# The last 64 features of gate and up on two halves of the rows, and a main loop dealt out by hand

## The chip, the cores and the metric

The kernel runs on one core of one Trainium2 chip. The metric is the device time of one execution in microseconds (us). A core has a matrix engine (TensorE, "PE" in the profile, with its weight loads as "PEld"), a vector engine (VectorE, "DVE"), a scalar engine (ScalarE, "ACT"), GpSimd ("POOL") and SyncE ("SP", which here only issues transfers). TensorE writes its results to PSUM, eight banks of 512 float32 values on each of 128 rows; ScalarE and VectorE move them from there to the on-chip memory.

## The reference

The kernel computes the output of a block and its gradients with respect to the inputs and weights. The block is an adaptive layer norm, a filter in the frequency domain, a second adaptive layer norm, and a gated layer without a nonlinearity:

```python
h = _layernorm(x) * (1 + ca) + sa
x = x + ga * irfft2(rfft2(h) * (w_r + 1j * w_i))
h = _layernorm(x) * (1 + cb) + sb
g = h @ w_gate; u = h @ w_up
x = x + gb * ((g * u) @ w_down)
```

There are 2048 tokens (16 tiles of 128), 576 features and 4608 hidden units (36 blocks of 128); data is bfloat16. The main loop belongs to the gated layer. With gh the gradient that comes back to the hidden units (grad_out scaled by gb, times w_down transposed), it computes g and u, then g * u, gh * u and gh * g, the three weight gradients, and the gradient of h.

## The kernel before

The program builds its instructions from Python loops; a scheduler then orders them by priority, which is program order unless said otherwise, and starts an instruction earlier when it is ready and others wait. Buffers come from pools with a fixed number of copies. A transfer is queued on SP or POOL, and each queue is worked off in order.

Before the main loop, the spectral stages and the product with w_down (u4p, L365) run. L495 makes h2p, the second normalised input with tokens on the rows; it has 640 columns, and L209 has filled the last 64 with zeros. L499 turns it by a transposing transfer into h2T: five blocks of 128 features on the rows, of which the fifth holds 64 features and 64 rows of zeros.

The main loop (L584 to L643) passes once over each of the 36 hidden blocks, fb. A pass has these parts:

- *gup* (L604 to L613): for four groups of 512 tokens and for gate and up, one PSUM bank is filled by five matmuls (L609), one for each block of features; the fifth has 64 rows of weights and 64 rows of zeros (L588). ScalarE copies the bank out (L610, gT and uT); VectorE makes hhT, ggT and guT (L611 to L613).
- *turn* (L614 to L620): hhT goes to memory, and three transposing transfers on SP (L619) make hh_sf, gg_sf and gu_sf, with tokens on the rows.
- *u57* (L548 to L569), for the block before: three weight gradients, each of two halves of 288 columns with 16 matmuls a half (L554), a copy by ScalarE (L556), and a store, for two of the three behind another transposing transfer (L561 to L563).
- *u8* (L627 to L640): for 16 token tiles and two halves, two matmuls (L635) and an addition by VectorE (L640) into a float32 sum. Pass 34 leaves this out, and pass 35 does both blocks, with four matmuls a bank.

So TensorE has 40 matmuls of 512 columns and 96 + 64 of 288 columns in a pass. PSUM is split three ways: three banks for gup, three for u8p, two for u57p. Weights of gate and up (wgu, two copies, each for two passes) come in on SP and POOL (L591, L592), the gradient ghh on POOL (L598), and turned weights wT every fourth pass (L578). The order of the parts on TensorE is the scheduler's: it mixes gup of the next pass with u8 of this one, and u57 runs in one piece. After the loop the two last blocks' u57 follow, among them the first matmuls of the next stage (L829), each tied behind an entry of the list "fill".

Of the kernel before, what the change touches and what calls it, by code (L numbers as in the profile page):

```python
# [9 lines left out]
FP32 = mybir.dt.float32  # L10
# [9 lines left out]
NT = 16  # L20
S = 2048
D = 576
# [60 lines left out]
def build(ctx, tc, A_x, A_w_r, A_w_i, B_w_gate, B_w_up, B_w_down, c_in, w_mod, grad_out,  # L83
# [103 lines left out]
    with ExitStack() as hs:  # L187
# [319 lines left out]
    with ExitStack() as ms:  # L507
# [13 lines left out]
        with ExitStack() as bs:  # L521
# [23 lines left out]
            nso = [0]  # L545
            fill = []

            def u57_product(sf, rhs_n):  # L548
                so = so4[:, nso[0] % NSO, :]
                nso[0] += 1  # L550
                for h in range(2):
                    pw = u57ps.tile([128, 512], FP32, name="u57p")
                    for t in range(NT):
                        mm = nc.tensor.matmul(pw[:, 0:288], lhsT=sf[:, t, :], rhs=rhs_n[:, t, h * 288:(h + 1) * 288], start=(t == 0), stop=(t == NT - 1))  # L554
                    fill.append(mm.ins)
                    nc.scalar.copy(so[:, h * 288:(h + 1) * 288], pw[:, 0:288])  # L556
                return so
# [7 lines left out]
            def emit_u57(fb_, sfs_):  # L565
                so = u57_product(sfs_[0], gon)
                nc.sync.dma_start(out_6[fb_ * 128:(fb_ + 1) * 128, :], so[:, 0:D])
                for sf, odst in ((sfs_[1], out_4), (sfs_[2], out_5)):
                    u57_turn(fb_, u57_product(sf, h2n), odst)  # L569

            def wT_load(f0, after):
                nb = min(FBT, NFB - f0)
# [6 lines left out]
                return wT  # L579

            wgu = None
            wTs = {}
            u8 = []
            for fb in range(NFB):  # L584
                if fb % FBW == 0:
                    nb = min(FBW, NFB - fb)
                    wgu = wp.tile([128, 2, 5, FBW * 128], BF, name="wgu")
                    nc.gpsimd.memset(wgu[64:128, :, 4, :], 0.0)  # L588
                    for wi_, wsrc in enumerate((B_w_gate, B_w_up)):
                        eng = nc.sync if wi_ == 0 else nc.gpsimd  # L590
                        eng.dma_start(wgu[:, wi_, 0:4, 0:nb * 128], wsrc[0:512, fb * 128:(fb + nb) * 128].rearrange("(m q) f -> q m f", q=128))  # L591
                        eng.dma_start(wgu[0:64, wi_, 4, 0:nb * 128], wsrc[512:576, fb * 128:(fb + nb) * 128])  # L592
                if fb == 0:
                    wTs[0] = wT_load(0, turns[-7:-2])
                jw = fb % FBW
                jt = fb % FBT
                ghh = ghp.tile([128, NT, 128], BF, name="ghh")
                nc.gpsimd.dma_start(ghh[:].rearrange("f t p -> f (t p)"), ghhT_d[fb * 128:(fb + 1) * 128, :])  # L598
                gT = tp2.tile([128, NT, 128], BF, name="gT")
                uT = tp2.tile([128, NT, 128], BF, name="uT")  # L600
                hhT = tp.tile([128, NT, 128], BF, name="hhT")
                ggT = tp.tile([128, NT, 128], BF, name="ggT")
                guT = tp.tile([128, NT, 128], BF, name="guT")
                for sb4 in range(4):  # L604
                    ts_ = slice(4 * sb4, 4 * sb4 + 4)
                    for wi_, dstT in enumerate((gT, uT)):
                        pt = gups.tile([128, 4, 128], FP32, name="gup")
                        for m in range(5):
                            nc.tensor.matmul(pt[:], lhsT=wgu[:, wi_, m, jw * 128:(jw + 1) * 128], rhs=h2T[:, ts_, m, :], start=(m == 0), stop=(m == 4))  # L609
                        nc.scalar.copy(dstT[:, ts_, :], pt[:])  # L610
                    nc.vector.tensor_tensor(out=hhT[:, ts_, :], in0=gT[:, ts_, :], in1=uT[:, ts_, :], op=MUL)  # L611
                    nc.vector.tensor_tensor(out=ggT[:, ts_, :], in0=ghh[:, ts_, :], in1=uT[:, ts_, :], op=MUL)
                    nc.vector.tensor_tensor(out=guT[:, ts_, :], in0=ghh[:, ts_, :], in1=gT[:, ts_, :], op=MUL)  # L613
                nc.gpsimd.dma_start(hhT_d[:, :, fb, :].rearrange("tp f x -> f tp x"), hhT[:].rearrange("f (tp ti) p -> f tp (ti p)", ti=2))  # L614
                sfs = []
                for nm, srcT in (("hh_sf", hhT), ("gg_sf", ggT), ("gu_sf", guT)):
                    sf = sfp.tile([128, NT, 128], BF, name=nm)
                    with tc.high_priority(-2 * HEAD_START if fb == NFB - 1 else 0):
                        turned = nc.sync.dma_start_transpose(out=sf[:], in_=srcT[:].rearrange("f t p -> f (t p)"))  # L619
                    sfs.append(sf)  # L620
                if fb % FBT == 1 and fb + 3 < NFB:
                    wTs[fb // FBT + 1] = wT_load(fb + 3, [turned.ins] * 5)
                wT = wTs[fb // FBT]
                if pend and fb < NFB - 1:
                    emit_u57(*pend.pop(0))
                u8.append((ggT, guT, wT, jt))
                for t in range(NT):  # L627
                    if fb == NFB - 2:
                        break
                    for h in range(2):  # L630
                        hs_ = slice(h * 288, (h + 1) * 288)
                        pu = u8ps.tile([128, 512], FP32, name="u8p")
                        mms = [(x[:, t, :], wt_[:, wi_, j_, hs_]) for gg_, gu_, wt_, j_ in u8 for wi_, x in enumerate((gg_, gu_))]
                        for k, (l_, r_) in enumerate(mms):
                            nc.tensor.matmul(pu[:, 0:288], lhsT=l_, rhs=r_, start=(k == 0), stop=(k == len(mms) - 1))  # L635
                        dst = acc(t)[:, hs_]
                        if fb == 0:
                            nc.vector.tensor_copy(dst, pu[:, 0:288])
                        else:
                            nc.vector.tensor_tensor(out=dst, in0=dst, in1=pu[:, 0:288], op=ADD)  # L640
                if fb != NFB - 2:
                    u8 = []
                pend.append((fb, sfs))  # L643
            fill.clear()
            for p in pend:
                emit_u57(*p)
        res2cm.__exit__(None, None, None)
        res3cm.__exit__(None, None, None)

# [506 lines left out]
```

## Time and profile before

| | us |
|---|---|
| median of 3 runs | 1622.52 |
| lowest, highest | 1619.5, 1630.39 |
| the profiled execution's own time | 1615.75 |
| its span, first to last instruction | 1614.0 |
| mean granted TensorE clock | 0.989 |

All lines of the profile are from that one execution. In the groups of instructions, a line names the source line, engine, operation, what is written and read, the shape and the count; then come the total busy time in us, the mean duration of one in ns, and the idle time of that engine just before such instructions with what ended it. Matmuls are pipelined, so their durations overlap: the sum over a group is not the time that it took, and the distance between two starts is. The main loop fills some 980 us of the span, from the first L609 at 280.0 us to the last at 1258.5.

### The profile page before, as it was taken

How to read it: one execution, taken by the hardware profiler on the slowest of the kernel's cores; microseconds unless marked ns; L12 is line 12 of the kernel's file. 1: busy time of each engine (PE TensorE's matmuls, PEld its weight loads, DVE VectorE, ACT ScalarE, POOL GpSimd, SP SyncE). 2: the span in 40 equal slices, each digit the busy share in tenths (PEclk: the TensorE clock that was granted, in tenths of full speed). 3: DMA queues.
4: the chain of work that ended last, by engine and by line, in shares of the span. 5: the costliest groups of instructions: out<-in, count | busy, mean ns of one | idle time of the engine just before them, and what ended most of it. 6: DMA issues, size and time to landing. Idle time of an engine off the chain costs nothing.

```text
span 1614.0 us, 29981 instructions
## 1 busy us (share of the span) xinstructions
PE 1558.2 (97%) x11354; PEld 1067.8 (66%) x11354; DVE 990.4 (61%) x2594; ACT 560.1 (35%) x1108; POOL 180.5 (11%) x303
## 2 busy tenths in 40 slices
PE   6999999999999999999999999999999889899996
PEld 4666644667666676766667676666767666677774
DVE  7766743674756657475665747566574765678655
ACT  6666722222222222222222222222222265565022
POOL 0002311101010100101010010101000011100232
PEclk9999999999999999999999999999999999999998
DMA  9978993777677685866867686786856686635774
GB/s 324 280 211 235 281 278 128 161 131 152 133 157 140 129 161 109 176 137 128 164 123 150 132 167 115 151 146 130 173 98 142 179 253 193 235 113 181 273 225 153
DMA packets 482996, 280.38 MB, mean 174 GB/s; under 512 B 405377, under 2 KB 450178, under 8 KB 481954
## 3 DMA queue, kind: packets, MB, share of 16 engines
q1 hardware_dynamic: 457666, 185.38, 53.2%
q0 software_dynamic: 25184, 93.07, 18.7%
q8 instruction: 89, 1.46, 0.4%
q14 instruction: 57, 0.47, 0.1%
HBM read 108.51 MB, written 82.31 MB: 118 GB/s over the span
## 4 chain that ended last, share of the span: by engine, by line
PE 81%; DMA 7%; DVE 5%; issue 3%; ACT 3%; SPq 0%; POOL 0%; ACTq 0%; DVEq 0%; POOLq 0%
PE u57p L554 26%; PE gup L609 19%; PE u8p L635 17%; PE u4p L365 9%; PE u3p L1056 2%; DMA Xn<-xn_d 2%; PE yp L472 1%; DMA n2c<-n_d 1%; DMA wdB<-in_B_w_down_dram 1%; PE zp L317 1%; DMA out_dram<-o 1%; PE zp L829 1%; PE yp L965 1%; DMA ghhT_d<-ghh_st 1%; DVE pr L746 1%
## 5 line engine op out<-in xcount | busy, mean ns | idle before, releaser
L640 DVE TENSOR_TENSOR acc<-acc,u8p 128x288 f32<-128x288 f32 x1088 | 429.5, 450 | 354.1 <-PE u8p L635 352.9
L609 PE MATMUL gup<-h2T,wgu 128*128 128x512 bf16 x1440 | 433.3, 379 | 0.6 <-ACT uT L610 0.6
L635 PE MATMUL u8p<-wT,ggT 128*128 128x288 bf16 x1152 | 315.0, 287 | 4.3 <-DVE acc L640 4.3
L635 PE MATMUL u8p<-wT,guT 128*128 128x288 bf16 x1152 | 315.1, 287 | 0.0
L609 PEld LDWEIGHTS <-wgu 128*128 128x128 bf16 x1440 | 140.8, 98 | 97.4 <-issue 0.8
L556 ACT CAST so<-u57p 128x288 bf16<-128x288 f32 x216 | 86.2, 399 | 328.5 <-PE u57p L554 324.3
L635 PEld LDWEIGHTS <-guT 128*128 128x128 bf16 x1152 | 112.8, 98 | 101.3 <-issue 4.7
L365 PE MATMUL u4p<-goT,wdT 128*128 128x512 bf16 x720 | 163.7, 382 | 2.7 <-ACT ghh_st L139 2.4
L610 ACT CAST gT<-gup 128x512 bf16<-128x512 f32 x144 | 84.4, 586 | 226.3 <-PE gup L609 226.3
L554 PE MATMUL u57p<-gon,hh_sf 128*128 128x288 bf16 x1152 | 151.0, 288 | 0.0
L610 ACT CAST uT<-gup 128x512 bf16<-128x512 f32 x144 | 84.4, 586 | 189.3 <-PE gup L609 186.7
L554 PE MATMUL u57p<-h2p,gu_sf 128*128 128x288 bf16 x1152 | 148.5, 286 | 0.0
L554 PE MATMUL u57p<-h2p,gg_sf 128*128 128x288 bf16 x1152 | 148.1, 286 | 0.0
L554 PEld LDWEIGHTS <-hh_sf 128*128 128x128 bf16 x1152 | 113.5, 99 | 35.8
L1056 PEld LDWEIGHTS <-hl 128*128 128x128 bf16 x1152 | 111.2, 98 | 35.9 <-issue 8.2
L635 PEld LDWEIGHTS <-ggT 128*128 128x128 bf16 x1152 | 112.9, 98 | 29.1
L554 PEld LDWEIGHTS <-gg_sf 128*128 128x128 bf16 x1152 | 112.5, 98 | 28.3
L554 PEld LDWEIGHTS <-gu_sf 128*128 128x128 bf16 x1152 | 112.5, 98 | 28.2
L365 PEld LDWEIGHTS <-wdT 128*128 128x128 bf16 x720 | 70.0, 98 | 80.9 <-issue 6.0
L1056 PE MATMUL u3p<-wdB,hl 128*128 128x288 bf16 x672 | 94.2, 287 | 7.0 <-DMA wdB<-in_B_w_down_dram 6.0
L614 POOL DMA_DIRECT2D hhT_d<-hhT x36 | 33.2, 922 | 502.8 <-DVE hhT L611 498.6
L611 DVE TENSOR_TENSOR hhT<-gT,uT 128x512 bf16<-128x512 bf16 x144 | 60.7, 421 | 29.5 <-ACT uT L610 27.1
(355 smaller groups left out, 1659.1 us busy)
## 6 DMA issues: line engine op xcount, KB each, us to landing
ghhT_d<-ghh_st POOLq DMA_DIRECT2D x36, 512.0 KB, 4.1
ghh<-ghhT_d POOLq DMA_DIRECT2D x36, 512.0 KB, 7.7
hhT_d<-hhT POOLq DMA_DIRECT2D x36, 512.0 KB, 6.7
hl<-hhT_d SPq DMA_DIRECT2D x32, 576.0 KB, 8.3
out_dram<-woT SPq DMA_DIRECT2D x72, 128.0 KB, 2.0
wdn<-in_B_w_down_dram SPq DMA_DIRECT2D x18, 288.0 KB, 3.7
out_dram<-so SPq DMA_DIRECT2D x36, 144.0 KB, 2.4
wgu<-in_B_w_gate_dram SPq DMA_DIRECT2D x18, 256.0 KB, 3.3
```

Source lines behind the costliest of these rows:

```text
L317: mm = nc.tensor.matmul(zp[:, :FP], lhsT=hTs[t][:, m, :], rhs=T["RD"][:, m, cc, :], start=(m == 0), stop=(m == 4))
L365: nc.tensor.matmul(pt[:], lhsT=wdTs[k][:, j, m, :], rhs=goT[:, 4 * sb4:4 * sb4 + 4, m, :], start=(m == 0), stop=(m == 4))
L472: nc.tensor.matmul(yp[:, 0:288], lhsT=ut[:, fc, cc * 128:(cc + 1) * 128], rhs=T["IR"][:, fc, cc, h * 288:(h + 1) * 288], start=(k == 0), s ...
L554: mm = nc.tensor.matmul(pw[:, 0:288], lhsT=sf[:, t, :], rhs=rhs_n[:, t, h * 288:(h + 1) * 288], start=(t == 0), stop=(t == NT - 1))
L556: nc.scalar.copy(so[:, h * 288:(h + 1) * 288], pw[:, 0:288])
L609: nc.tensor.matmul(pt[:], lhsT=wgu[:, wi_, m, jw * 128:(jw + 1) * 128], rhs=h2T[:, ts_, m, :], start=(m == 0), stop=(m == 4))
L610: nc.scalar.copy(dstT[:, ts_, :], pt[:])
L611: nc.vector.tensor_tensor(out=hhT[:, ts_, :], in0=gT[:, ts_, :], in1=uT[:, ts_, :], op=MUL)
L614: nc.gpsimd.dma_start(hhT_d[:, :, fb, :].rearrange("tp f x -> f tp x"), hhT[:].rearrange("f (tp ti) p -> f tp (ti p)", ti=2))
L635: nc.tensor.matmul(pu[:, 0:288], lhsT=l_, rhs=r_, start=(k == 0), stop=(k == len(mms) - 1))
L640: nc.vector.tensor_tensor(out=dst, in0=dst, in1=pu[:, 0:288], op=ADD)
L1056: mm = nc.tensor.matmul(p2[:, 0:288], lhsT=hls[fb // 9][:, fb % 9, ti * 128:(ti + 1) * 128], rhs=(wdA[:, fb] if fb < 15 else wdB[:, fb - 1 ...
```

## The change

**The fifth block on two halves of the rows.** The zeros in h2p are replaced by a second copy of features 512 to 575 (a VectorE addition of 64 columns beside L495), so that the fifth block of h2T holds these features on rows 0 to 63 and again on rows 64 to 127. The weights' tile becomes nine blocks: four of gate, four of up, and one in which gate's last 64 features lie on rows 0 to 63 and up's on rows 64 to 127. The fill of L588 goes.

**Four short matmuls open a batch of four banks.** A pass has two batches ("half" 0 and 1), each of two token groups for gate and up. A batch first issues four matmuls over 64 rows, one for each bank, gate and up in turn, and then for each bank the four whole blocks. Three banks come from gup's, the fourth from u57p's pool.

**The rest dealt by hand.** Each pass writes a list of small steps: first batch, third weight gradient of block fb - 2, second batch, turn, first and second weight gradient of block fb - 1. Between these steps the 32 u8 outputs of block fb - 1 are dealt out evenly. A weight gradient is now one step for each matmul. The last two blocks' u8 and u57 follow the loop, as before.

```diff
-        nc.gpsimd.memset(h2p[:, :, D:DP], 0.0)
...
+                nc.vector.tensor_tensor(out=h2p[:, s0 + i, D:DP], in0=nm[:, 512:D], in1=modh[MSB][:, 512:D], op=ADD)
...
-            def u57_product(sf, rhs_n):
+            def u57_items(sf, rhs_n, done):
...
+                    def item(h, t, pw=pw):
+                        if t == 0:
+                            pw.append(u57ps.tile([128, 512], FP32, name="u57p", tag="x"))
+                        mm = nc.tensor.matmul(pw[0][:, 0:288], lhsT=sf[:, t, :], rhs=rhs_n[:, t, h * 288:(h + 1) * 288], start=(t == 0), stop=(t == NT - 1))
+                        if t == NT - 1:
+                            fill.append(mm.ins)
+                            nc.scalar.copy(so[:, h * 288:(h + 1) * 288], pw[0][:, 0:288])
...
+            def gup_items(fb, half):
...
+                def corners():
+                    for sb4 in (2 * half, 2 * half + 1):
+                        for wi_ in range(2):
+                            r = slice(64 * wi_, 64 * wi_ + 64)
+                            pts.append((u57ps if len(pts) == 3 else gups).tile([128, 4, 128], FP32, name="gup", tag="x"))
+                            nc.tensor.matmul(pts[-1][:], lhsT=wgu[r, 8, jw * 128:(jw + 1) * 128], rhs=h2T[r, 4 * sb4:4 * sb4 + 4, 4, :], start=True, stop=False)
+
+                def item(k, m):
+                    sb4, wi_ = 2 * half + k // 2, k % 2
+                    ts_ = slice(4 * sb4, 4 * sb4 + 4)
+                    nc.tensor.matmul(pts[k][:], lhsT=wgu[:, 4 * wi_ + m, jw * 128:(jw + 1) * 128], rhs=h2T[:, ts_, m, :], start=False, stop=(m == 3))
...
+                return [corners] + [lambda k=k, m=m: item(k, m) for k in range(4) for m in range(4)]
...
-                    wgu = wp.tile([128, 2, 5, FBW * 128], BF, name="wgu")
-                    nc.gpsimd.memset(wgu[64:128, :, 4, :], 0.0)
+                    wgu = wp.tile([128, 9, FBW * 128], BF, name="wgu")
...
+                        eng.dma_start(wgu[64 * wi_:64 * wi_ + 64, 8, :], wsrc[512:576, fb * 128:(fb + FBW) * 128])
...
-                for sb4 in range(4):
-                    ts_ = slice(4 * sb4, 4 * sb4 + 4)
-                    for wi_, dstT in enumerate((gT, uT)):
-                        pt = gups.tile([128, 4, 128], FP32, name="gup")
-                        for m in range(5):
-                            nc.tensor.matmul(pt[:], lhsT=wgu[:, wi_, m, jw * 128:(jw + 1) * 128], rhs=h2T[:, ts_, m, :], start=(m == 0), stop=(m == 4))
...
+                main = gup_items(fb, 0)
+                if fb >= 2:
+                    main += product(fb - 2, 2)
+                main += gup_items(fb, 1)
+                turn_at = len(main)
+                main.append(turn_items(fb))
+                if 1 <= fb < NFB - 1:
+                    main += product(fb - 1, 0) + product(fb - 1, 1)
+                outs = [(fb - 1, t, h) for t in range(NT) for h in range(2)] if 1 <= fb < NFB - 1 else []
+                dealt = 0
+                for k, f in enumerate(main):
+                    f()
+                    while dealt < len(outs) * (k + 1) // len(main):
+                        u8_output([outs[dealt][0]], *outs[dealt][1:])
+                        dealt += 1
```

More of the change, by code (lines that the diff above doesn't have):

```diff
@@ L546, in build @@
             fill = []
-            def u57_product(sf, rhs_n):
+            def u57_items(sf, rhs_n, done):
                 so = so4[:, nso[0] % NSO, :]
                 nso[0] += 1
+                items = []
                 for h in range(2):
[L552 to L557, printed above, removed]
+                    pw = []
+                    def item(h, t, pw=pw):
[5 more added lines that the diff above has]
+                            nc.scalar.copy(so[:, h * 288:(h + 1) * 288], pw[0][:, 0:288])
+                            if h == 1:
+                                done(so)
+                    items += [lambda h=h, t=t, item=item: item(h, t) for t in range(NT)]
+                return items
             def u57_turn(fb_, so, odst):
@@ L563, in u57_turn, with product, done @@
                 nc.sync.dma_start(odst[512:576, fb_ * 128:(fb_ + 1) * 128], woT[0:64, 4, :])
[L565 to L569, printed above, removed]
+            def product(fb_, i):
+                odst = (None, out_4, out_5)[i]
+                def done(so):
+                    if i:
+                        u57_turn(fb_, so, odst)
+                    else:
+                        nc.sync.dma_start(out_6[fb_ * 128:(fb_ + 1) * 128, :], so[:, 0:D])
+                return u57_items(sfs[fb_][i], h2n if i else gon, done)
             def wT_load(f0, after):
@@ L581, in build @@
             wgu = None
-            wTs = {}
-            u8 = []
+            wTs, sfs, trip = {}, {}, {}
+            def gup_items(fb, half):
+                jw = fb % FBW
+                gT, uT, hhT, ggT, guT, ghh, wgu = trip[fb]
+                pts = []
+                def corners():
[8 more added lines that the diff above has]
+                    nc.tensor.matmul(pts[k][:], lhsT=wgu[:, 4 * wi_ + m, jw * 128:(jw + 1) * 128], rhs=h2T[:, ts_, m, :], start=False, stop=(m == 3))
+                    if m == 3:
+                        nc.scalar.copy((gT, uT)[wi_][:, ts_, :], pts[k][:])
+                    if m == 3 and wi_ == 1:
+                        nc.vector.tensor_tensor(out=hhT[:, ts_, :], in0=gT[:, ts_, :], in1=uT[:, ts_, :], op=MUL)
+                        nc.vector.tensor_tensor(out=ggT[:, ts_, :], in0=ghh[:, ts_, :], in1=uT[:, ts_, :], op=MUL)
+                        nc.vector.tensor_tensor(out=guT[:, ts_, :], in0=ghh[:, ts_, :], in1=gT[:, ts_, :], op=MUL)
+                return [corners] + [lambda k=k, m=m: item(k, m) for k in range(4) for m in range(4)]
@@ new lines, in turn_items, with turns_ @@
+            def turn_items(fb):
+                def turns_():
+                    hhT, ggT, guT = trip[fb][2:5]
+                    nc.gpsimd.dma_start(hhT_d[:, :, fb, :].rearrange("tp f x -> f tp x"), hhT[:].rearrange("f (tp ti) p -> f tp (ti p)", ti=2))
+                    sfs[fb] = []
+                    for nm, srcT in (("hh_sf", hhT), ("gg_sf", ggT), ("gu_sf", guT)):
+                        sf = sfp.tile([128, NT, 128], BF, name=nm)
+                        with tc.high_priority(-2 * HEAD_START if fb == NFB - 1 else 0):
+                            turned = nc.sync.dma_start_transpose(out=sf[:], in_=srcT[:].rearrange("f t p -> f (t p)"))
+                        sfs[fb].append(sf)
+                    if fb % FBT == 1 and fb + 3 < NFB:
+                        wTs[fb // FBT + 1] = wT_load(fb + 3, [turned.ins] * 5)
+                return turns_
@@ new lines, in u8_output @@
+            def u8_output(fbs, t, h):
+                hs_ = slice(h * 288, (h + 1) * 288)
+                pu = u8ps.tile([128, 512], FP32, name="u8p")
+                mms = [(x[:, t, :], wTs[fb // FBT][:, wi_, fb % FBT, hs_]) for fb in fbs for wi_, x in enumerate(trip[fb][3:5])]
+                for k, (l_, r_) in enumerate(mms):
+                    nc.tensor.matmul(pu[:, 0:288], lhsT=l_, rhs=r_, start=(k == 0), stop=(k == len(mms) - 1))
+                dst = acc(t)[:, hs_]
+                if fbs[0] == 0:
+                    nc.vector.tensor_copy(dst, pu[:, 0:288])
+                else:
+                    nc.vector.tensor_tensor(out=dst, in0=dst, in1=pu[:, 0:288], op=ADD)
@@ L584, in build @@
             for fb in range(NFB):
                 if fb % FBW == 0:
-                    nb = min(FBW, NFB - fb)
-                    wgu = wp.tile([128, 2, 5, FBW * 128], BF, name="wgu")
-                    nc.gpsimd.memset(wgu[64:128, :, 4, :], 0.0)
+                    wgu = wp.tile([128, 9, FBW * 128], BF, name="wgu")
                     for wi_, wsrc in enumerate((B_w_gate, B_w_up)):
                         eng = nc.sync if wi_ == 0 else nc.gpsimd
-                        eng.dma_start(wgu[:, wi_, 0:4, 0:nb * 128], wsrc[0:512, fb * 128:(fb + nb) * 128].rearrange("(m q) f -> q m f", q=128))
-                        eng.dma_start(wgu[0:64, wi_, 4, 0:nb * 128], wsrc[512:576, fb * 128:(fb + nb) * 128])
+                        eng.dma_start(wgu[:, 4 * wi_:4 * wi_ + 4, :], wsrc[0:512, fb * 128:(fb + FBW) * 128].rearrange("(m q) f -> q m f", q=128))
+                        eng.dma_start(wgu[64 * wi_:64 * wi_ + 64, 8, :], wsrc[512:576, fb * 128:(fb + FBW) * 128])
@@ L593, in build @@
                 if fb == 0:
                     wTs[0] = wT_load(0, turns[-7:-2])
-                jw = fb % FBW
-                jt = fb % FBT
                 ghh = ghp.tile([128, NT, 128], BF, name="ghh")
                 nc.gpsimd.dma_start(ghh[:].rearrange("f t p -> f (t p)"), ghhT_d[fb * 128:(fb + 1) * 128, :])
-                gT = tp2.tile([128, NT, 128], BF, name="gT")
-                uT = tp2.tile([128, NT, 128], BF, name="uT")
-                hhT = tp.tile([128, NT, 128], BF, name="hhT")
@@ L602, in build @@
-                ggT = tp.tile([128, NT, 128], BF, name="ggT")
-                guT = tp.tile([128, NT, 128], BF, name="guT")
-                for sb4 in range(4):
-                    ts_ = slice(4 * sb4, 4 * sb4 + 4)
-                    for wi_, dstT in enumerate((gT, uT)):
-                        pt = gups.tile([128, 4, 128], FP32, name="gup")
-                        for m in range(5):
[L609 to L640, printed above, removed]
@@ L641, in build @@
-                if fb != NFB - 2:
-                    u8 = []
-                pend.append((fb, sfs))
+                trip[fb] = [p.tile([128, NT, 128], BF, name=nm) for p, nm in ((tp2, "gT"), (tp2, "uT"), (tp, "hhT"), (tp, "ggT"), (tp, "guT"))] + [ghh, wgu]
+                main = gup_items(fb, 0)
[4 more added lines that the diff above has]
+                main.append(turn_items(fb))
@@ new lines, in build @@
+                if 1 <= fb < NFB - 1:
[7 more added lines that the diff above has]
+                        dealt += 1
+            for t in range(NT):
+                for h in range(2):
+                    u8_output([NFB - 2, NFB - 1], t, h)
@@ L644, in build @@
             fill.clear()
-            for p in pend:
-                emit_u57(*p)
+            for fb_ in (NFB - 2, NFB - 1):
+                for i in range(3):
+                    for f in product(fb_, i):
+                        f()
         res2cm.__exit__(None, None, None)
```

## The prediction

> **What bounds the kernel now.** I read the page's busy times first, then the chain of waits, then two stretches of the main loop, then the groups of the loop and the timeline at its start.
>
> ```profile
> PE 1558.2 (97%) x11354; PEld 1067.8 (66%) x11354; DVE 990.4 (61%) x2594; ACT 560.1 (35%) x1108; POOL 180.5 (11%) x303
> ...
> PE u57p L554 26%; PE gup L609 19%; PE u8p L635 17%; PE u4p L365 9%; PE u3p L1056 2%; DMA Xn<-xn_d 2%; PE yp L472 1%; DMA n2c<-n_d 1%; DMA wdB<-in_B_w_down_dram 1%; PE zp L317 1%; DMA out_dram<-o 1%; PE zp L829 1%; PE yp L965 1%; DMA ghhT_d<-ghh_st 1%; DVE pr L746 1%
> ```
>
> TensorE is named at three lines of the main loop with 62% of the span. The chain of waits in order of time gives the rhythm of the loop:
>
> ```profile
> 414.96 4.10 PE gup L609 x19
> 419.06 11.76 PE u57p L554 x96
> ...
> 443.21 4.10 PE gup L609 x19
> ...
> 1250.23 8.63 PE gup L609 x40
> ```
>
> One pass lasts 443.21 - 414.96 = 28.25 us. 96 matmuls of 288 columns take 11.76 us, 0.1225 us each; 40 of 512 columns take 8.63 us, 0.2157 us each. A pass holds 40 of the latter (L609) and 96 + 64 of the former (L554, L635): 8.63 + 160 x 0.1225 = 28.23 us, against 28.25. So TensorE issues without a gap. The stretches (PE, PEld, DVE, ACT and POOL busy, then clock and DMA share) say the same, at full clock:
>
> ```profile
> 414.96:443.21 28.25, 28.25 (x201) 19.55 (x200) 16.86 (x45) 7.08 (x14) 3.23 (x5) 1.00 0.70 142
> 443.21:471.47 28.26, 28.26 (x202) 19.56 (x200) 16.89 (x45) 7.08 (x14) 1.48 (x2) 1.00 0.74 161
> ```
>
> In this loop a matmul slot taken away is worth its full spacing, and order alone can win nothing.
>
> ```profile
> L609 PE MATMUL gup<-h2T,wgu 128*128 128x512 bf16 x1440 | 433.3, 379 | 0.6 <-ACT uT L610 0.6
> L640 DVE TENSOR_TENSOR acc<-acc,u8p 128x288 f32<-128x288 f32 x1088 | 429.5, 450 | 354.1 <-PE u8p L635 352.9
> ...
> L609 PEld LDWEIGHTS <-wgu 128*128 128x128 bf16 x1440 | 140.8, 98 | 97.4 <-issue 0.8
> ```
>
> A matmul of L609 is 0.379 us long but follows the last one after 0.2157: 0.163 us of its end lies under the next. A weight load is 0.098 us and lies under the matmul before it. These are the covers that the change can break.
>
> **The change, part by part.**
>
> *Fewer slots.* Of a pass's 40 matmuls, 8 (the fifth block of each bank) carry 64 real rows of 128. After, gate's lie on rows 0 to 63 and up's on 64 to 127. If two such run side by side, the 8 cost 4 spacings. Saved: 4 x 0.2157 = 0.863 us a pass, 36 passes: 31.1 us.
>
> *Switches.* Short matmuls come four at a time, twice a pass: 72 batches, so 144 changes between whole-height and half-height work. Every PE row of the trace is 128*128, so none shows this price. Lower bound: zero, since going from 512 to 288 columns costs nothing (28.23 against 28.25); a switch has no way to gain. Next: the first half-height matmul waits until the last whole one has left, 0.163 us. Highest: the weight load isn't hidden either. Its distance to its matmul is 0.12 us here:
>
> ```profile
> 713.09 0.10 PEld L635 LDWEIGHTS <-ggT 128*128 128x128 bf16 x1
> 713.21 0.29 PE L635 MATMUL u8p<-wT,ggT 128*128 128x288 bf16 x1
> ```
>
> That makes 0.163 + 0.12 = 0.283 us. Break-even is 31.1 / 144 = 0.216 us. I take 0.08, the middle of zero and the tail: a pipeline that empties overlaps part of its tail with the next operand's way in. 144 x 0.08 = 11.5 us; ends 0 and 40.8.
>
> The Trainium skill (TensorEngine Tiling (Array Packing), Key Properties) says that changing the tiling mode, not just the tile, drains the engine. It gives no time for that; by it the switch is at least the tail, the rival "drain" below, and no run here shows it yet.
>
> *Second of a pair.* It starts with the first at best, one weight load (0.098 us) later at worst. I take 0.025, since a load already hides under a running matmul: 72 x 0.025 = 1.8 us; ends 0 and 7.1. The Trainium skill (TensorE: Matmul & The Clock Gate, Measured speedup vs the span model) has matmuls on separate row tiles start about 4 ns apart, which as an estimate would make this 0.3 us; no run here shows it.
>
> *Start of the loop.* ScalarE's second copy waits for a store of the stage before:
>
> ```profile
> 284.40 0.59 ACT L610 CAST uT<-gup 128x512 bf16<-128x512 f32 x1 [2.53 <-DMA ghhT_d<-ghh_st]
> ...
> 285.04 4.48 PE L609 MATMUL gup<-h2T,wgu 128*128 128x512 bf16 x20 [0.55 <-ACT uT L610]
> ```
>
> TensorE loses 0.55 us there. After, the first half is done some 18 spacings after 280.0, at 283.9, and the next batch wants four banks at once, the third of them free after two more copies, at 285.6. Loss 1.7 - 0.55, about 1.1 us, once. The end of the loop keeps its 128 + 192 matmuls; only 32 of pass 33 move into the last pass: 0.
>
> *Dealt order.* Covers: 131 steps share 32 outputs, so an L640 addition of 0.45 us is due every 27.4 / 32 = 0.86 us, with three u8p banks. DVE's whole pass is 32 x 0.45 + 12 x 0.42 (L611 to L613) = 19.4 us of 27.4. If that cover went, TensorE would wait at L635 for L640. The transposes (SP, L619, up to 8.4 us of issue and 13.2 to landing) have about one pass before L554 reads them, much as now (one of hh_sf is issued at 704.1 and read from 729.9). SP's queue keeps its order by passes: the weights of L591 and L592 still wait for a buffer two passes back; the two result stores and transposes of a product wait behind the three L619 transposes, and only the four-deep ring of so waits on them. A batch's fourth bank comes from u57p, whose last copy but one (0.40 us) is over 16 matmuls earlier. All at zero.
>
> *Small edits.* Eighteen fills of wgu (0.52 us, POOL) and one of h2p (0.94 us) go; nobody waits for them, and the POOL load behind L588 waits for the same TensorE read. Sixteen 64-wide additions join L495: by the nearest rows 0.22 us (128x64, L880) to 0.45 (L495 itself), 3.5 to 7.2 us of DVE, where TensorE is busy 68.9 of 70 us (140 to 210) and L365 work is queued until 280. Cost zero; 7 us if the cover went.
>
> *Sum.* -31.1 + 11.5 + 1.8 + 1.1 = -16.7 us. The profiled execution took 1615.75 us (span 1614.0 and 1.75 around it), 6.8 below the median of the runs, 1622.52; taken off that median, 1605.8 us.
>
> **The rivals.**
>
> *Drain and reload:* each switch costs 0.163 to 0.283 us. For it: the trace has whole-height work alone, so nothing in it shows that a half-height load may run under it. Against it: loads and tails are covered at every other change of shape. Gain 28.2 - 144 s: +4.7 to -12.6 us, 1618 to 1635; at its middle 1626. The Trainium skill's page TensorEngine Tiling (Array Packing), section Key Properties, states the rule behind this rival.
>
> *In a row, the slower side:* the short matmuls of a pair do not overlap, because the second's load or its bank waits for the first; a batch then takes four spacings, 0.863 us, and saves nothing, while its two switches still cost the tail: 144 x 0.163 = 23.5, plus 1.1: 1647 us. It decides if the second starts about 0.22 us after the first; with no overlap a switch of 0.11 us is enough to lose over 1%. For it: PE's records never show two matmuls starting together. Against it: the two use other rows, other weights and other banks.
>
> *It doesn't do what it says:* half-height matmuls run as whole ones, eight spacings, no switch: 1623 us. Then the short ones would stand at 0.2157 like any other.
>
> **How the numbers follow.** The forecast (switch between zero and the tail) gets 0.74, drain and reload 0.09, in a row 0.14, no effect 0.03. A measurement here can tell about 1%, 16.2 us, from no change. Within the forecast the gain runs from 28.2 to 4.7 us and passes 16.2 at a switch of (28.2 - 16.2) / 144 = 0.083 us, the middle: 0.41 of its 0.74 faster, as the change out of a batch has its loads hidden as now, and 0.33 within. Faster 0.41; within 0.33 + 0.09 + 0.03 = 0.45; slower 0.14. The likeliest case's own range is 1594 to 1618. With no cost at the pairs or the start and the scatter of the runs (3 us down to 1619.5) the low end is 1590; upwards it reaches through the other cases to 1630, the middle of drain and reload and 4 us of scatter. What is left out is the slow end of that rival and "in a row".
>
> **What would show it.** A pass 0.16 to 0.81 us shorter than 28.25 (0.863 less four switches and two pair offsets) by the distance between two like matmuls. In the timeline of a batch: second short matmul within 0.1 us of the first, the third one spacing (0.216) after the first, and before the first and behind the fourth a hole between zero and 0.16 us. PE busy per pass then stays a little under its length. Wrong if a hole is over 0.22, if the shorts stand 0.216 apart, if L635 waits for L640 or L609 for L610 in every pass, or if u57p waits for an L619 transpose.

## The result, and the profile after

The changed kernel took 1611.72 us (median of 7 runs) beside 1628.47 for the kernel before on the same chip: a ratio of 0.9896, 95% interval 0.9858 to 0.9934. Two more comparisons on other chips gave 0.987 (0.9827 to 0.9914) and 0.9857 (0.9818 to 0.9896). So the change is worth some 17 to 23 us; 16.7 were forecast. The forecast time, 1605.8 us, lies 5.9 us under the measured one because the kernel before itself took 6 us more than in the runs that the forecast started from (1628.47 and 1622.52).

The changed kernel's profiled execution took 1611.72 us as well (span 1609.9). Its busy times and its chain of waits by line:

```profile
PE 1542.1 (96%) x11354; PEld 1041.0 (65%) x11354; DVE 1038.4 (65%) x2610; ACT 559.1 (35%) x1108; POOL 170.4 (11%) x284
...
PE u57p L558 25%; PE u8p L640 17%; PE gup L611 15%; PE u4p L364 7%; DMA ghhT_d<-ghh_st 2%; PE gup L606 2%; PE u3p L1091 2%; DMA Xn<-xn_d 2%; DMA n2c<-n_d 1%; DMA wdB<-in_B_w_down_dram 1%; DMA xc<-in_A_x_dram 1%; DMA x1t<-x_d 1%; PE yp L471 1%; PE zp L316 1%; PE yp L1000 1%
```

In the new numbering L606 are the short matmuls, L611 the whole ones of gate and up, L613 ScalarE's copies, L558 u57, L640 u8, L645 its additions. TensorE still carries the loop: gate and up fall from 19% to 15 + 2%. The transfer ghhT_d<-ghh_st has grown from 1% to 2%; more of it below.

One pass, as a stretch between like matmuls (length, busy times of PE, PEld, DVE, ACT, POOL, then clock, DMA share, GB/s):

```profile
444.03:471.83 27.80, 27.80 (x202) 18.86 (x202) 18.27 (x44) 7.08 (x14) 1.45 (x2) 1.00 0.69 130
```

A pass is 27.80 us (the next one 27.79) where it was 28.25: 0.45 less, inside the forecast 0.16 to 0.81. PE counts as busy through all of it, holes included, since a record of 288 columns lasts 0.29 us; the forecast that it would stay a little under the length of a pass did not hold. One batch in the timeline (start, duration, engine, line, operation, tile, shape, count; what the engine waited for, in brackets):

```profile
693.36 0.29 PE L640 MATMUL u8p<-wT,guT 128*128 128x288 bf16 x1
693.58 0.60 PE L606 MATMUL gup<-h2T,wgu 64*128 64x512 bf16 x4
694.12 1.04 PE L611 MATMUL gup<-h2T,wgu 128*128 128x512 bf16 x4
```

```profile
693.57 0.11 PEld L606 LDWEIGHTS <-wgu 64*128 64x128 bf16 x4 [0.24 <-issue]
694.11 0.55 PEld L611 LDWEIGHTS <-wgu 128*128 128x128 bf16 x4 [0.42 <-issue]
```

The first short matmul comes 0.22 us after the last 288-column one, whose spacing is 0.1225: a hole of 0.10. From the first short to the first whole one are 0.54 us: two spacings of 0.2157 and again 0.11. So the two of a pair run side by side, with no offset that this view of 0.01 us can show (the trace's own records, in ns, have the second 3 or 4 ns behind the first), and a switch costs about 0.104 us each way. The holes stand in the loads' row too, 0.24 and 0.42 us before the first load of each height: elsewhere a load starts with the matmul before it, here with its own. A hole is also about as long as a load (0.098 us); whether the load fills it, or the last matmul's way out, no run here separates. This gives a pass of 28.25 - 0.863 + 4 x 0.104 = 27.80.

Three stretches of the profiled executions of before and after, in us, by first and last matmul of gate and up and last of u57:

| | before | after |
|---|---|---|
| start of the loop | 280.0 | 298.1 |
| loop | 978.5 | 963.2 |
| loop's end to the last u57 | 98.7 | 92.5 |
| from there to the end | 256.8 | 256.1 |

The first row is a time from the start of the span, to the first short matmul after; the others are lengths. The loop gives 15.3 us and the stretch behind it 6.2; the loop starts 18 us later, which the forecast did not have. The experiments take these three apart.

### The profile page after: what moved, and what is told of

Read it like the earlier page. It is cut to its first block, busy times and chain, and to the rows that moved or that the text cites. A ratio compares the mean times of both kernels' runs of the same rounds, so it can differ in the third digit from the quotient of the medians.

```text
span 1609.9 us, 29989 instructions
## 1 busy us (share of the span) xinstructions
PE 1542.1 (96%) x11354; PEld 1041.0 (65%) x11354; DVE 1038.4 (65%) x2610; ACT 559.1 (35%) x1108; POOL 170.4 (11%) x284
## 4 chain that ended last, share of the span: by engine, by line
PE 77%; DMA 11%; DVE 5%; ACT 3%; issue 3%; POOL 0%; SPq 0%; DVEq 0%; ACTq 0%; POOLq 0%
PE u57p L558 25%; PE u8p L640 17%; PE gup L611 15%; PE u4p L364 7%; DMA ghhT_d<-ghh_st 2%; PE gup L606 2%; PE u3p L1091 2%; DMA Xn<-xn_d 2%; DMA n2c<-n_d 1%; DMA wdB<-in_B_w_down_dram 1%; DMA xc<-in_A_x_dram 1%; DMA x1t<-x_d 1%; PE yp L471 1%; PE zp L316 1%; PE yp L1000 1%
## 5 line engine op out<-in xcount | busy, mean ns | idle before, releaser
L645 DVE TENSOR_TENSOR acc<-acc,u8p 128x288 f32<-128x288 f32 x1088 | 488.6, 453 | 315.1 <-PE u8p L640 314.7
L640 PE MATMUL u8p<-wT,ggT 128*128 128x288 bf16 x1152 | 327.5, 286 | 1.2 <-DVE acc L645 1.2
L640 PE MATMUL u8p<-wT,guT 128*128 128x288 bf16 x1152 | 327.2, 286 | 0.0
L611 PE MATMUL gup<-h2T,wgu 128*128 128x512 bf16 x1152 | 295.4, 379 | 0.0
L558 PE MATMUL u57p<-gon,hh_sf 128*128 128x288 bf16 x1152 | 188.6, 286 | 0.2 <-DMA hh_sf<-hhT 0.2
L558 PE MATMUL u57p<-h2p,gg_sf 128*128 128x288 bf16 x1152 | 187.6, 286 | 0.0
L558 PE MATMUL u57p<-h2p,gu_sf 128*128 128x288 bf16 x1152 | 186.3, 286 | 0.0
L611 PEld LDWEIGHTS <-wgu 128*128 128x128 bf16 x1152 | 109.5, 98 | 98.9 <-issue 17.5
L640 PEld LDWEIGHTS <-ggT 128*128 128x128 bf16 x1152 | 112.6, 98 | 67.2 <-issue 14.0
L640 PEld LDWEIGHTS <-guT 128*128 128x128 bf16 x1152 | 112.7, 98 | 55.3 <-issue 1.8
L364 PEld LDWEIGHTS <-wdT 128*128 128x128 bf16 x720 | 70.2, 99 | 98.1 <-issue 23.6
L558 PEld LDWEIGHTS <-hh_sf 128*128 128x128 bf16 x1152 | 112.6, 98 | 28.8 <-DMA hh_sf<-hhT 0.5
L558 PEld LDWEIGHTS <-gu_sf 128*128 128x128 bf16 x1152 | 112.5, 98 | 28.4
L558 PEld LDWEIGHTS <-gg_sf 128*128 128x128 bf16 x1152 | 112.5, 98 | 28.3
L613 ACT CAST gT<-gup 128x512 bf16<-128x512 f32 x144 | 84.4, 586 | 129.7 <-PE gup L611 129.7
L613 ACT CAST uT<-gup 128x512 bf16<-128x512 f32 x144 | 84.3, 585 | 75.9 <-PE gup L611 73.0
L141 DVE CAST ghh_st<-u4p 128x512 bf16<-128x512 f32 x56 | 38.7, 690 | 75.0 <-PE u4p L364 55.4
```

The source lines that it names most:

```text
L141: nc.vector.tensor_copy(dst, src)
L364: nc.tensor.matmul(pt[:], lhsT=wdTs[k][:, j, m, :], rhs=goT[:, 4 * sb4:4 * sb4 + 4, m, :], start=(m == 0), stop=(m == 4))
L558: mm = nc.tensor.matmul(pw[0][:, 0:288], lhsT=sf[:, t, :], rhs=rhs_n[:, t, h * 288:(h + 1) * 288], start=(t == 0), stop=(t == NT - 1))
L611: nc.tensor.matmul(pts[k][:], lhsT=wgu[:, 4 * wi_ + m, jw * 128:(jw + 1) * 128], rhs=h2T[:, ts_, m, :], start=False, stop=(m == 3))
L613: nc.scalar.copy((gT, uT)[wi_][:, ts_, :], pts[k][:])
```

## The experiments

The theory: each change between whole and half height costs TensorE 0.104 us, pairs on two halves cost one spacing, and this alone makes the loop's gain. Rivals: the gain comes from the dealt order; the price belongs to the batch and not to the switch. Two further questions: where do the 6 us after the loop come from, and is the late start the change's doing?

**Both kernels again**, unedited.

> The kernel before, unchanged, for a second trace. Main loop: one pass 28.25 us, as in the first trace. Theory A (the 18 us by which the changed kernel's main loop started later are a chance delay of transfers in the stage before it, which both kernels meet): TensorE waits at u4p for ghh_st of anything from 2 to 18 us, and more than the 2.4 us of the first trace, since the timed runs were 4 to 15 us longer than the profiled one. Theory B (the change makes that delay): 2 to 3 us of such waits again and the loop's first L609 near 280 us.

Before again: 1628.34 us, ratio 0.9997 (0.997 to 1.0024); loop 978.5, start 279.4, behind it 99.9.

> The changed kernel, unchanged, for a second trace. One pass 27.80 us, each batch of four short matmuls 0.64 us by the spacing (two spacings of 0.2157 and two switches of 0.104). Theory A: the wait at u4p for ghh_st differs from the 18 us of the first trace by several us, and the span follows it. Theory B: again 15 to 20 us of waits and a loop that starts near 298 us.

After again: 1607.85 us, 0.987; loop 963.5, start 293.5, behind it 93.6. The loops repeat to 0.3 us, the other stretches to a few.

**The dealt order without the half height.** The fifth block keeps 128 rows with zeros, with a block of weights each for gate and up, all else as in the changed kernel:

```diff
...
-                            nc.tensor.matmul(pts[-1][:], lhsT=wgu[r, 8, jw * 128:(jw + 1) * 128], rhs=h2T[r, 4 * sb4:4 * sb4 + 4, 4, :], start=True, stop=False)
+                            nc.tensor.matmul(pts[-1][:], lhsT=wgu[:, 8 + wi_, jw * 128:(jw + 1) * 128], rhs=h2T[:, 4 * sb4:4 * sb4 + 4, 4, :], start=True, stop=False)
...
+                    nc.gpsimd.memset(wgu[64:128, 8:10, :], 0.0)
...
```

> The changed kernel, but the fifth block is whole again: eight matmuls over 128 rows with 64 rows of zero weights, dealt in the same order. If the gain comes from the half-height matmuls alone: one pass 28.25 us (40 x 0.2157 + 160 x 0.1225 = 28.23) and 16 us more than the changed kernel in the loop. If the dealt order gives something itself: below 28.2. If the dealt order costs something: above 28.3.

1622.13 us, ratio 0.9959 (0.9921 to 0.9997): 6.4 us below before. A pass is 28.23 us, the loop 977.9. The dealt order wins 0.6 us in the loop, next to nothing. Behind it 93.4 us, as after: the 6 us of that stretch belong to the order.

**All short matmuls on rows 0 to 63**, so that no two can run side by side (up's weights move to a block of their own):

```diff
-                            r = slice(64 * wi_, 64 * wi_ + 64)
+                            r = slice(0, 64)
...
```

> The changed kernel, but both gate's and up's last 64 features lie on rows 0 to 63: the same number of short matmuls and switches, no two on different rows. If pairs run side by side only because of their rows: four spacings a batch, so a pass of 28.25 + 4 x 0.104 = 28.67 us, 31 us over the changed kernel in the loop, shorts 0.216 us apart. If short matmuls are cheap for another reason (half the rows take half the time): 27.80 as in the changed kernel.

1639.69 us, 1.0075 (1.0049 to 1.0101). In the chain of waits a batch of this kernel and then one of the changed kernel:

```profile
706.69 0.97 PE gup L606 x4
```

```profile
454.21 0.54 PE gup L606 x4
```

0.97 is four spacings (0.863) and the exit's 0.10; 0.54 is two and the same 0.10. Sharing the array is worth 0.43 us a batch, and the price of a switch does not depend on it. The loop takes 992.7 us, 29.5 more than after, where 31 were expected.

**Batches of two.** Twice as many switches in a pass, the same pairs:

```diff
...
-                return [corners] + [lambda k=k, m=m: item(k, m) for k in range(4) for m in range(4)]
+                return [f for b in range(2) for f in [lambda b=b: corners(b)] + [lambda k=k, m=m: item(k, m) for k in (2 * b, 2 * b + 1) for m in range(4)]]
```

> The change with its short matmuls in batches of two (one bank of gate and one of up) instead of four, all else as in the changed kernel. The program then has 146 steps of one spacing and 292 changes between short and whole matmuls, twice as many as before this edit. Theory 'a fixed price of each change between short and whole work' (0.104 us each way, read from the changed kernel's batches; the two of a pair side by side): shorts cost 146 x 0.2157 + 292 x 0.104 = 61.9 us, where the 288 slots of the kernel before cost 62.1, so the loop gains nothing: a pass 28.2 to 28.3 us, the loop some 14 us longer than the changed kernel's 963, the whole time 14 us above the changed kernel, about 1622 (with the 6 us that the order at the end of the loop gives). Rival 'the price belongs to the batch, not to the change' (a fixed hole of 0.1 us per batch and only one of the two ends): pass 27.9 to 28.0, about 1615. Rival 'no price worth the name, the gain comes from the dealt order': pass 27.8 as now, about 1608.

1616.7 us, 0.9959 (0.9928 to 0.9991). Two like pieces of its chain, one pass apart:

```profile
696.39 0.75 PE gup L611 x3
...
724.61 0.75 PE gup L611 x3
```

28.22 us; the model says 28.25 - 0.863 + 8 x 0.104 = 28.22. The loop is 977.3, 14.1 longer than after, where 14 were expected. So the price goes with each switch, not with the batch, and batches of two give all of the loop's saving back. The 6.7 us that the ratio still gives over before agree with the dealt order's 6.

**The half height without the dealt order.** Before's loop, in which one short matmul of gate and one of up open each pair of banks, and the scheduler places them:

```diff
...
+                    for wi_ in range(2):
+                        r = slice(64 * wi_, 64 * wi_ + 64)
+                        pts.append(gups.tile([128, 4, 128], FP32, name="gup"))
+                        nc.tensor.matmul(pts[-1][:], lhsT=wgu[r, 8, jw * 128:(jw + 1) * 128], rhs=h2T[r, ts_, 4, :], start=True, stop=False)
...
-                        for m in range(5):
+                        for m in range(4):
...
```

> The kernel before with its own loop and the scheduler's order, and only the fifth block on two halves of the rows: the short matmul of gate and the short matmul of up open each pair of banks. The scheduler sets other work between most of them: 206 short ones stand alone and 41 in pairs, 494 changes between short and whole work. Theory 'fixed price of each change, 0.104 us': 247 x 0.2157 + 494 x 0.104 = 104.7 us in place of 62.1, so the loop is 42 us longer than the 978.5 of before, a pass 29.4 us, the whole time about 1670 against 1628 (6 us less if the order at the end of the loop also comes out as in the changed kernel). Rival 'no price for a change': 8.9 us gained, about 1620. Rival 'price as I took it before the run, 0.08 us': about 1658.

1665.05 us, 1.024 (1.0208 to 1.0272). In its chain L609 is the short one:

```profile
707.58 0.32 PE gup L609
```

0.32 us is one spacing and one switch, 0.2157 + 0.104; most stand alone, with other work between. The loop is 1020.5 us, 42.0 longer than before; 42 were expected. One price fits the loops of all four kernels with half-height work to within 1.5 us. And the run shows what the hand-dealt order is for: the same arithmetic, left to this scheduler, costs 39 us where the change gains some 20.

**The 16 additions alone**, in the kernel before:

```diff
-        nc.gpsimd.memset(h2p[:, :, D:DP], 0.0)
...
+                nc.vector.tensor_tensor(out=h2p[:, s0 + i, D:DP], in0=nm[:, 512:D], in1=modh[MSB][:, 512:D], op=ADD)
```

> The kernel before with one part of the change alone: 16 additions of 64 columns in place of the fill of the last 64 columns (the weights' zeros stay, so the result is the same). In all four profiles of kernels with the change the first whole matmul of gate and up starts at 288 to 299 us, in both of before at 280. Theory 'chance: the transposes and loads of the stage before collide differently in each execution, and the profiles of before caught two early ones': the start is between 279 and 283 in this profile or, if late, late in a profile whose time is no worse than before's median, and the ratio of the timed runs is 1.000 within 0.003 (1628 us). Theory 'the additions delay the transposes of h2 and make the loop start late': start at 288 or later, the timed runs 5 to 12 us slower than before. Theory 'POOL's queue does it' (other instructions on POOL without the fills): no change here, but one in the run with the later loads.

1627.56 us, 1.0006 (0.9983 to 1.003), start at 283.0. They cost nothing that can be measured and do not make the loop start late.

**The late start.** In the waits of TensorE between 130 us and the loop, the changed kernel's profile has this (in total, times, longest), and before's this:

```profile
PE u4p L364 <- ACT ghh_st L139: 15.6, 2, 13.8
```

```profile
PE u4p L365 <- ACT ghh_st L139: 2.4, 1, 2.4
```

ScalarE cannot write ghh_st until its store by POOL has left. POOL's loads for the main loop are queued among these stores, and in the changed kernel's profile one of them stood for an earlier load of wgu, with the stores behind it:

```profile
POOL wgu L653 <- DMA wgu<-in_B_w_up_dram: 10.7, 1, 10.7
```

So these loads were put behind the store of block 27, in the changed kernel:

```diff
...
+                        with tc.issue_after(stored4[27]) if wi_ else ExitStack():
...
+                with tc.issue_after(stored4[27]):
                     nc.gpsimd.dma_start(ghh[:].rearrange("f t p -> f (t p)"), ghhT_d[fb * 128:(fb + 1) * 128, :])
```

> The changed kernel with POOL's loads for the main loop (weights of up, ghh of the first two blocks) queued behind the store of block 27 of ghh, so that the stores of the stage before don't wait behind them. Theory 'POOL's queue makes the loop start late': TensorE's waits between 130 us and the loop's start fall from 16 to 20 us to 8 or less, the loop starts at 279 to 286 instead of 294 to 298, and the timed runs are 8 to 15 us below the changed kernel, about 1597. Theory 'the transposes of h2 and the DMA engines of that stage set it, whatever is queued on POOL': start at 290 or later, time as the changed kernel, 1608 within 4. In either case a pass stays at 27.80 us.

1600.19 us, 0.9838 (0.9812 to 0.9864); start 282.4, waits 7.1 us. Then once more beside the unedited changed kernel, and the same edit in the kernel before:

> The changed kernel with POOL's loads for the loop behind the store of block 27, again, to have its time beside the changed kernel's on one chip. Theory 'POOL's loads hold up the stores of the stage before': TensorE's waits before the loop 8 us or less, loop start 279 to 286, time 6 to 14 us below the changed kernel. Theory 'chance': within 3 us of the changed kernel.

> The changed kernel once more, beside the next two on one chip: 1608 us within 4, a pass of 27.80 us. Theory 'the late start belongs to the change': TensorE's waits between 130 us and the loop's start are again 13 us or more and the loop starts at 290 or later, as in all earlier profiles with the change and with the dealt order. Theory 'chance': this profile can as well show 4 to 8 us and a start near 282.

> The kernel before with the same edit on POOL (its loads for the loop behind the store of block 27); no other queue and no other engine gets another order. Theory 'the stall is met by both kernels in ordinary runs, and the profiles of before show early ones': 5 to 12 us faster than before, 1616 to 1622. Theory 'the stall belongs to the change alone': same time as before, 1.000 within 0.003, since its profiles show waits of 4 to 5 us there. A pass stays at 28.25 us.

With the edit 1597.97 us, 0.9829 (0.9798 to 0.986), start 282.2; the changed kernel 1601.81, 0.9857 (0.9818 to 0.9896), start 291.5, waits 12.7; the kernel before with the edit 1618.71, 0.9967 (0.9943 to 0.999), start 277.7. In the profiles of the second run with the edit, and then of the changed kernel beside it, the row reads:

```profile
PE u4p L364 <- ACT ghh_st L139: 6.1, 3, 5.6
```

```profile
PE u4p L364 <- ACT ghh_st L139: 8.9, 1, 8.9
```

By the timed runs the old places of these loads cost time in both kernels: the edit takes 5.3 us from before. From the changed kernel it takes about 4 to 5 here, with intervals that overlap; this size is not settled. The row alone does not settle it either: it holds 3.2 and 3.0 us in the profiles with one half of the rows and with batches of two, which start late as well. Against "the change alone" speaks that the three ratios of the changed kernel fit the loop (15.3) and the stretch behind it (about 6) with nothing lost at the start. Against "chance" speaks that every profile with the dealt order and POOL's old places starts at 288 to 304 us (seven) and every one in before's order at 278 to 284 (five). But the profiled executions in before's order ran 2 to 13 us below the medians of their runs, and five of the seven with the dealt order 5 to 16 us above, so the profiles overstate the difference. Why they part so clearly and the timed ones do not stays open.

**The stretch behind the loop.** SP's queue at the loop's end, before and then after (start, time of issue):

```profile
1260.97 5.04 SPq L619 DMA_TRANSPOSE hh_sf<-hhT  x1
1266.10 0.64 SPq L778 DMA_DIRECT2D n2c<-n_d  x1
```

```profile
1264.83 0.52 SPq L813 DMA_DIRECT2D n2c<-n_d  x1
...
1276.50 4.01 SPq L629 DMA_TRANSPOSE hh_sf<-hhT  x1
```

Before, the next stage's first load (n2c) stands behind a transpose that takes 5 us to issue. VectorE's queue then shows who pays, and TensorE's after it:

```profile
1264.56 1.65 DVE L640 TENSOR_TENSOR acc<-acc,u8p 128x288 f32<-128x288 f32 x4
1270.57 0.76 DVE L795 SCALAR_TENSOR_TENSOR jk<-gn,n2c 128x576 bf16<-128x576 bf16 x1 [4.37 <-DMA n2c<-n_d]
```

```profile
1267.02 0.41 PE L554 MATMUL u57p<-gon,hh_sf 128*128 128x288 bf16 x2
1271.76 0.40 PE L635 MATMUL u8p<-wT,ggT 128*128 128x288 bf16 x1 [4.33 <-DVE acc L640]
1271.96 0.44 PE L635 MATMUL u8p<-wT,guT 128*128 128x288 bf16 x1
1272.20 0.44 PE L635 MATMUL u8p<-wT,ggT 128*128 128x288 bf16 x1
```

VectorE waits at L795, the u8p additions queue behind it, and TensorE stands for 4.33 us. The test: the changed kernel with n2c behind hh_sf again, every other order its own:

```diff
...
-            ld, gyTs, zts = {"order": []}, {}, {}
+            ld, gyTs, zts = {"order": [hh_last[-1]]}, {}, {}
```

> The changed kernel with the last transpose of hh_sf queued on SP ahead of the next stage's first loads (n2c), as it stands in the kernel before; SP's order around the end of the loop is then that of before, every other order that of the changed kernel. Theory 'the later n2c holds up VectorE, behind it the additions of u8p, and so TensorE': TensorE's wait at the u8p matmuls for the additions is again 4 to 5 us (1.2 to 2.0 in the changed kernel, 4.3 to 5.4 in before), the granted clock 10 to 20 us after the last whole matmul of gate and up falls to 0.66 to 0.83, and last gup to last u57 takes 97 to 100 us, 4 to 6 more than in the changed kernel; the timed runs 3 to 6 us above it. Rival 'the 6 us of the tail come from elsewhere (other transfers, the clock by chance)': the wait stays below 2 us and the time is the changed kernel's.

1611.4 us, 0.9891 (0.9854 to 0.9929), beside 0.9857 for the changed kernel in the same comparison: some 5 us back, with overlapping intervals. The waits of TensorE behind the loop, in the changed kernel and then in this one:

```profile
PE u8p L640 <- DVE acc L645: 1.2, 2, 0.7
```

```profile
PE u8p L642 <- DVE acc L647: 4.8, 1, 4.8
```

The wait is back, and the stretch takes 100.9 us instead of 92.5 to 93.9. (Its profiled execution is 16 us above its median, with 23.6 us of waits before the loop; only the end is read here.) Not all of this stretch is that order: with POOL's loads later it took 98.0 and 96.3 us at a wait of 1.6 and 1.3. There TensorE's granted clock stood at half for 10.2 us of the stretch, in the three profiles of the changed kernel for 3.4 to 6.8; the last section has more on that.

## Why the prediction was right, step by step

- *What bounds the kernel*: right. A slot taken away shortened the loop, and the dealt order without it won 0.6 us there.
- *Fewer slots, -31.1*: right in size. The scheduler split some batches at the start of the loop, so the 288 short matmuls cost 147 spacings and not 144: -30.4.
- *Switches, 0.08 us each, +11.5*: right in place, too low. 0.104 us, 151 of them inside the loop: +15.7. Together -14.7, measured -15.3; the dealt order's 0.6 is the rest. "Drain and reload" was a rival with 0.163 to 0.283; the price lies below it. The rule of the Trainium skill (TensorEngine Tiling (Array Packing), Key Properties) that a change of mode drains the engine agrees with the hole at each switch, though a load that is no longer covered would leave the same hole; the prediction's reading of the rule, at least the whole 0.163 us tail, does not.
- *Second of a pair, 0.025 us*: too high; the trace's records have 3 or 4 ns. The Trainium skill's 4 ns (TensorE: Matmul & The Clock Gate, Measured speedup vs the span model) agree with that.
- *In a row*: fallen. The run on one half of the rows has what this rival described, and it is 1.0075 of before, at 1639.69 us on its chip.
- *Start of the loop, +1.1*: the waits at L610 are gone, and the split batches above stand in their place: three spacings and eight switches more, 1.5 us. The later start in the profile was not forecast; the timed runs do not charge it to the change.
- *End of the loop and dealt order, 0*: wrong. The prediction asked of SP's queue only whether the transposes come in time, not what of the next stage is queued behind the last one. Worth about 6 us.
- *Small edits, 0*: right by the run with the additions alone. Each took 0.186 us, under the 0.22 taken as its lower bound.

So the gain is near the forecast 16.7 for two reasons: the loop gains 15.3, a little under the 17.8 that slots, switches and pairs were given, and the end adds some 6 that were given nothing. Of the three comparisons the first lies on the forecast gain, the other two 4 to 7 us beyond it. The mechanism in the loop was right; that the first comparison comes within 0.1 us of the forecast is luck, since the end of the loop was missed and the three comparisons spread over 6 us. The low end of the forecast's range comes out at 1588 and not 1590 from its own terms (31.1 saved and 3 of scatter), which changes nothing here.

## What to carry to other kernels

Half-height matmuls on two halves of the rows halve the cost of a half-empty block, but each change of height costs, here, half a spacing of a 512-column matmul (0.104 of 0.2157 us). Count the switches first: batches of four paid, batches of two gained nothing in the loop, scattered ones lost 39 us. Where an order is dealt anew, look also at what the next stage has queued behind the loop's last transfers.

The fastest kernel here is the change with POOL's loads behind the store of block 27: 0.9838 and 0.9829 of before.

## What was not expected of the hardware

The stall of TensorE at the loop's end is paid twice. Behind the 4.33 us wait above, the matmuls of 288 columns stand 0.24 us apart instead of 0.1225, until about 1277.5. The stretches of before say so in the clock's column, at 0.50 and then 0.75:

```profile
1271.76:1276.04 4.28, 4.28 (x19) 2.60 (x19) 3.87 (x12) 1.62 (x2) 0.00 (x0) 0.50 1.10 430
1276.04:1279.12 3.08, 3.08 (x20) 2.20 (x19) 2.51 (x8) 0.40 (x1) 0.00 (x0) 0.75 0.91 382
```

That is 4.28 x 0.5 + 3.08 x 0.25 = 2.9 us more. Together with a wait of 4.3 instead of 1.2 it makes 6.0 of the 6.2 us between 98.7 and 92.5. That is no fixed price: in the second profile of before the half clock behind the same wait (4.7 us there) lasted 3.4 us instead of 6.8 and cost 1.6 us. Later in the stretch TensorE waits for n2c again in both kernels (4.4 us at the longest before, 5.1 after) and runs at half clock behind it, for 6.8 us before and 3.4 after. These two differences cancel in part. The changed kernel's clock stays at 1.00 where before's fell first, and falls to 0.50 in its stall before the loop:

```profile
220.00:230.00 10.00, 1.11 (x3) 0.40 (x3) 1.75 (x5) 1.07 (x2) 1.42 (x3) 0.50 1.32 78
...
1271.30:1281.30 10.00, 9.50 (x77) 7.32 (x75) 9.55 (x28) 5.00 (x8) 0.00 (x0) 1.00 1.09 342
```

The Trainium skill (TensorE: Matmul & The Clock Gate, What's actually happening) says that the clock drops to half after an idle window of about 3.4 us and comes back after a busy one of that length. The 4.33 us here and the 0.7 us that left it at 1.00 agree, and so do the lengths: between 30 us and the last instructions of these traces the clock stands at half for 3.41 us or a multiple of it. That the whole window must be idle does not hold here. The clock also fell behind a wait of 2.42 us in before (at 212.6 us; TensorE was busy for 0.99 of the 3.41 us ahead of it) and behind one of 2.58 us in the changed kernel (at 207.7 us, 1.01 of 3.41).
